# Routing one group later, row transposes in four pieces, and plain loads on SyncE's queue, in an attention-then-experts kernel

## The chip, the cores and the metric

The kernel runs on one core of a Trainium2 chip. The metric is the device time of one execution in microseconds (us). Engines are called as the profile calls them: PE is TensorE, DVE is VectorE, ACT is ScalarE, POOL is GpSimd, SP is SyncE. SP computes nothing here; it issues DMAs and waits for semaphores. A "q" behind an engine's name in a row (SPq, PEq) means its instruction queue.

## The reference

```python
u, v: (8, 2496, 256)   z: (8, 2496, 64)          # float32
scores = (1 / S) * z @ z.T                        # per batch, S = 2496
x = u * (max(scores, 0) ** 2 @ v)                 # 19968 tokens of 256
logits = (x / |x|) @ (emb / |emb|).T / tau        # 8 experts
e = argmax(logits);  gate = softmax(logits)[e]
out = gate * (max(x @ w1[e], 0) @ w2[e])          # w1: 256x1024, w2: 1024x256 for each expert
```

Products are made in float16 with each operand split in a high and a low part, so that three matmuls give nearly float32.

## The kernel before, in words

There are two stages. The first is attention with routing. It runs over 8 batches, in each over 5 groups of queries (512 tokens, the last one 448), and in each group over 20 steps, one for every 128 keys. A step of a group does up to three things: `scores` (L270, L271) makes a 128x512 block of scores on PE; ACT turns it into the squared relu `a` (L273, L274); `parts` (L307, L308) splits it on DVE into the float16 tile `hl`; and `values` (L362 to L371) multiplies `hl` with the split keys' values `vv` into the group's accumulators `acc`. The score matrix is symmetric, so blocks below the diagonal are not computed again: `parts` transposes `hl` by a DMA on SP's queue (L320 into `tt`, L322 into `joint`), and a later group reads it. `hl` has five buffers, and `parts` works two steps ahead of `values`. A step with its own scores takes PE 1.75 us, one that reads `tt` 1.31 us.

When a group's 20 steps are done, `route` returns a list of small functions, its routing. The main loop calls one of them after each step of the next group (`queue.pop(0)()`, L1101). In order they are: `gate_x` (L409, x = acc * u), `square` (L420), `root`, `scale`, `split` (L446, L447: x as high and low float16 into `row`), a DMA transpose of all rows of the group (L450), `logits` (L464, 16 small matmuls on PE into `pt`), `norms` and `top` (L468 on, DVE reads `pt`), `exps`, `gates`, `rank` (PE), `place`, and `scatters` (L532, four indirect DMAs on POOL's queue, which write each token's row into `xs`, sorted by expert). Before the change the first function is called right behind the group, splits end after step 5 of the next group, logits come after step 11, their first reading by DVE after step 13 and the scatters after step 18.

The accumulators of group g lie in two PSUM banks, `a0` and `a1` for an even group, `a2` and `a3` for an odd one. `pt`, the logits of group g, takes the first of the same group's banks (`bank`, L404), after `gate_x` has emptied it; the group g + 2 accumulates in it next.

During a batch, the loop also prepares the next one: `ahead` (L1009) loads parts of z and v for their largest values (`scan_load`), and z for its split (`z_load`, `z_split`, `z_copy`); `v_load` loads v four steps before `v_split` needs it. `weights` (L558) turns each expert's weights into split float16: two loads of 1 MB (L563, L564), a scale, four `part`s, two stores of 1 MB (L627) into `wsd`. These plain loads and stores go through POOL's queue; only those of the first group go through SP's (`loader`, L101).

The second stage takes the sorted rows in slots of 256 or 128 tokens of one expert: SP loads weights (L919, L921) and row transposes (L896), PE makes the up and down products, POOL scatters the results (L970). Routing of the last groups goes on beside its first slots.

PE's instructions stay in the order in which the program names them. The other engines' order, and that of SP's queue in the first stage, is made by a planner, which simulates the program with costs of its own and issues on every engine what is ready first there. On the chip each engine then keeps that order: an instruction that waits holds up all behind it on its engine.

Of the kernel before, what the change touches and what calls it, by code (L numbers as in the profile page):

```python
# [19 lines left out]
P = 128  # L20
TA, TB = 256, 128
ROW = 260
ROWT = 320
EUP = 14
VAHEAD = 4
LOOK = 3
# [19 lines left out]
def relu2_attention_then_moe(ctx, tc, zT, u, v, emb, tau, w1, w2, ident, tri, iota_e, out):  # L46
# [51 lines left out]
    assert SP * DQ == ZSCANS * SCAN * P and DQ % ZSCANS == 0 and SP % VSCANS == 0  # L98
    scan = {}

    def loader(b, g=0):  # L101
        return nc.sync if b == 0 and g == 0 else nc.gpsimd

    def scan_load(b, what, i, eng=None):

        t = wk.tile([P, SCAN], F32, name="scan", tag="scan", bufs=2)
        if what == "z":
            src = zT[b, i * (DQ // ZSCANS):(i + 1) * (DQ // ZSCANS), :]
        else:
            src = v[b, i * (SP // VSCANS):(i + 1) * (SP // VSCANS), :]  # L110
        (eng or loader(b)).dma_start(t, src.rearrange("a c -> (a c)").rearrange("(p w) -> p w", p=P))
        scan[b, what, i] = t

    def scan_max(b, what, i):
# [58 lines left out]
    def z_load(b, c0):  # L173
        zt = zpool.tile([P, ZC], F32, name="zt", tag="zt", bufs=3)
        c1 = min(c0 + ZC, SP)
        m = P if b == 0 else DQ
        loader(b).dma_start(zt[:m, :c1 - c0], zT[b, :m, c0:c1])
        zraw[b, c0] = zt

    def z_split(b, c0):  # L180
# [14 lines left out]
    def z_copy(b, c0, c1):  # L195
        z1, z2 = Zs[b]
        c = slice(c0, c1)
        loader(b).dma_start(z1[DQ:P, c], z2[0:DQ, c])
        loader(b).dma_start(z2[DQ:P, c], z1[0:DQ, c])

    vraw = {}

    def v_load(b, s):
        vt = wk.tile([P, D], F32, name="vt", tag="vt", bufs=VAHEAD + 2)
        loader(b).dma_start(vt, v[b, s * P:(s + 1) * P, :])  # L205
        vraw[b, s] = vt

    VC = 4
# [19 lines left out]
    def v_split(b, s):  # L228
        vt = vraw.pop((b, s))
        vv = vring.tile([P, 2 * D], F16, name="vv", tag="vv")  # L230
        k = scan[b, "cv"]
        if s == NST - 1:

            lo, hi = slice(0, DQ), slice(DQ, P)
            vh = wk.tile([P, D], F16, name="vh", tag="vh", bufs=1)
            nc.scalar.activation(vv[lo, 0:D], vt[lo], AF.Copy, scale=k[lo])
            nc.vector.tensor_copy(vv[lo, D:], vv[lo, 0:D])
            nc.scalar.activation(vh[hi], vt[hi], AF.Copy, scale=k[hi])
            nc.vector.scalar_tensor_tensor(vv[hi, 0:D], vt[hi], k[hi], vh[hi], op0=ALU.mult, op1=ALU.subtract)
            nc.vector.memset(vv[hi, D:], 0.0)  # L240
        else:
            nc.scalar.activation(vv[:, 0:D], vt, AF.Copy, scale=k)
            nc.vector.scalar_tensor_tensor(vv[:, D:], vt, k, vv[:, 0:D], op0=ALU.mult, op1=ALU.subtract)
        Vs[b, s] = vv
# [128 lines left out]
    def u_load(b, g):  # L373
        t0, n = groups[g]
        ut = rt.tile([P, 4, D], F32, name="ut", tag="ut")
        m = n // P
        loader(b, g).dma_start(ut[:, :m, :], u[b, t0:t0 + m * P, :].rearrange("(j p) d -> p j d", p=P))
        if n > m * P:
            for h in range(2):
                loader(b, g).dma_start(ut[h * DQ:(h + 1) * DQ, m, :], u[b, t0 + m * P:t0 + n, :])  # L380
        return ut

    obs = [cst.tile([P, 9, E], BF16, name=f"ob{i}") for i in range(2)]
    rows = [cst.tile([P, 4, ROWT], F32, name=f"row{i}") for i in range(2)]
    for t in obs:
        nc.gpsimd.memset(t, 0.0)
    for t in rows:
# [2 lines left out]
    def route(b, g, acc, ut):  # L390
# [48 lines left out]

        def split(j):  # L440
            up = loc["up"][:, j:j + 1]
            if j == 0:
                with tc.issue_after(loc["gate"]):
                    nc.vector.memset(row[:, :, D:D + 2], 0.0)
            hi, lo = row16[:, j, 0:D], row16[:, j, D:2 * D]
            nc.scalar.activation(hi, x[:, j, :], AF.Copy, scale=up)  # L446
            nc.vector.scalar_tensor_tensor(lo, x[:, j, :], up, hi, op0=ALU.mult, op1=ALU.subtract)  # L447
            if j == nj - 1:
                loc["rt"] = rt.tile([P, 4, ROWT * 2 // P, P], F16, name="rowt", tag="x", bufs=1)
                nc.sync.dma_start_transpose(loc["rt"].rearrange("p j i t -> p (j i) t"), row16.rearrange("p j c -> p (j c)"))  # L450

        def splits(j0):
            def f():
                for j in range(j0, min(j0 + 2, nj)):
                    split(j)
            return f

        def logits():
            pt = loc["pt"] = bank()
# [69 lines left out]
        def scatter(j):  # L529
            def f():  # L530
                m = min(P, n - j * P)
                put = nc.gpsimd.indirect_dma_start(  # L532
                    xs[:, :], bass.IndirectOffsetOnAxis(ap=loc["dsti"][:m, j:j + 1], axis=0),
                    row[:m, j, 0:ROW], None)
                for o in (o for old in puts.values() for o in old):
                    tc.declare_no_dep(put.ins, o, reason="each token has one row of xs")
                puts.setdefault(b, []).append(put.ins)
            return f
# [5 lines left out]
        def both(*fs):  # L544
# [4 lines left out]

        assert nj == 4  # L550
        none = lambda: None
        two = lambda j: both(lambda: square(j), lambda: square(j + 1))
        start = [gate_x, both(fold, two(0)) if n == 512 else none, two(2) if n == 512 else both(fold, two(0))]
        return start + [none if n == 512 else two(2), root, both(scale, splits(0)), splits(2)] + [none] * 5 + [
            logits, none, both(norms, top), exps, gates, rank, place, scatters]


    def weights(e):  # L558
        loc = {}

        def load():
            loc["wr"] = (wp.tile([P, W1], F32, name="wr1", tag="wr1"), wp.tile([P, W2], F32, name="wr2", tag="wr2"))
            nc.gpsimd.dma_start(loc["wr"][0].rearrange("p (k f) -> p k f", k=2), w1[e].rearrange("(k p) f -> p k f", p=P))  # L563
            nc.gpsimd.dma_start(loc["wr"][1].rearrange("p (k d) -> p k d", k=NF), w2[e].rearrange("(k p) d -> p k d", p=P))  # L564

        def maxes(k):
            def f():
# [22 lines left out]
        def powers():  # L590
            dg = loc["dg"]
            pm2 = psM.tile([P, 512], F32, name="pm", tag="m")
            nc.tensor.matmul(pm2[:, 0:2], ones_f[0:2, :], dg, start=True, stop=True)
            pw = sml.tile([P, 2], F32, name="pw")
            nc.vector.tensor_copy(pw, pm2[:, 0:2])
            up = sml.tile([P, 2], F32, name="wup")
            dn = sml.tile([P, 2], F32, name="wdn")
            for k, a in ((0, 2), (1, 9)):
                nc.vector.tensor_scalar(up.bitcast(I32)[:, k:k + 1], pw.bitcast(I32)[:, k:k + 1], -1.0,
                                        float((254 + a) << 23), op0=ALU.mult, op1=ALU.add)  # L600
                nc.vector.tensor_scalar(dn.bitcast(I32)[:, k:k + 1], pw.bitcast(I32)[:, k:k + 1], 1.0,
                                        float(-(a << 23)), op0=ALU.mult, op1=ALU.add)
            tail = sml.tile([P, 4], F32, name="tail")
            nc.gpsimd.memset(tail, 0.0)
            nc.vector.tensor_tensor(tail[:, 0:1], dn[:, 0:1], dn[:, 1:2], op=ALU.mult)
            nc.gpsimd.dma_start(wsd[e, :, WR1 + 2 * W2:], tail.bitcast(F16))
            loc["up"] = up

        def part(i):

            def f():
                k = i // 2
                wr = loc["wr"][k]
                W = (W1, W2)[k]
                if i % 2 == 0:
                    loc["wo"] = wp.tile([P, 2 * max(W1, W2)], F16, name="wo", tag="wo")
                wo = loc["wo"]
                u = loc["up"][:, k:k + 1]
                c = 512
                for o in range((i % 2) * (W // 2), (i % 2 + 1) * (W // 2), c):  # L620
                    m = min(c, (i % 2 + 1) * (W // 2) - o)
                    src = wr[:, o:o + m]
                    nc.scalar.activation(wo[:, o:o + m], src, AF.Copy, scale=u)
                    nc.vector.scalar_tensor_tensor(wo[:, W + o:W + o + m], src, u, wo[:, o:o + m],
                                                   op0=ALU.mult, op1=ALU.subtract)
                if i % 2 == 1:
                    nc.gpsimd.dma_start(wsd[e, :, 2 * k * W1:2 * (k * W1 + W)], wo[:, 0:2 * W])  # L627
            return f

        return [load, lambda: None, maxes(0), maxes(1), scales, powers] + [part(i) for i in range(4)]  # L630
# [402 lines left out]
    for i, (b, g, q, s) in enumerate(steps):  # L1033
# [75 lines left out]
            slot_weights()  # L1109
            slot_first()  # L1110
        if q == NST - 1:
            while queue:
                queue.pop(0)()
            queue = route(b, g, accs.pop((b, g)), uts.pop((b, g)))
            if b == B - 2 and g == NG - 1 and KA:
                queue.append(table_a)
            queue.pop(0)()
        if own:
            if nd + LOOK - 1 < len(direct):
# [98 lines left out]
```

## Time and profile before

| | us |
|---|---|
| median of 3 runs | 2328.91 (2327.23 to 2343.7) |
| the profiled execution | 2333.62 |
| its span, first to last instruction | 2331.8 |
| attention with routing, 25.4 to 1476.5 | 1451.1 |
| idle time of PE in it | 156.0 |
| of it, logits waiting for the transposed rows | 111.5 |
| expert stage, 1505 to 2331 | 826.0 |
| idle time of PE in it | 7.7 |

The profile is of one execution. Times in rows are in us from the start of the span unless marked ns. A row of a group of instructions has line, engine, operation, output and inputs by the program's names and a count. A row of a wait has who waited, for whom, total us, times, longest. A row of the timeline has start, duration, engine, line and operation; in brackets the idle time of the engine before it and what ended that. DMA rows tell packets, megabytes and, for each queue (q1 is SP's, q0 is POOL's), the time its packets took as a share of 16 DMA engines.

### The profile page before, as it was taken

The page shows a single profiled execution, that of the slowest core. Times are in us where ns is not written, and L with a number is a line of the kernel's source. Part 1 is how long each engine was busy: PE and PEld are TensorE (multiplying, and loading weights), DVE is VectorE, ACT ScalarE, POOL GpSimd, SP SyncE. Part 2 cuts the span into 40 slices and gives each one's busy share as a digit, 9 for nine tenths or more (in the row PEclk, how much of TensorE's full clock was granted, in tenths as well). Part 3 has the DMA queues.
Part 4 walks back from the last instruction along what each step waited for, and adds up shares of the span by engine and source line. Part 5 has one row for each costly group of instructions (what it writes and reads, how often), then busy time and mean ns, then how long its engine had stood idle before and what let it go on. Part 6 is the DMA issues. An engine that isn't in the chain of part 4 may idle for free. (4 is left out here: it accounts for less than half of the span.)

```text
span 2331.8 us, 50551 instructions
## 1 busy us (share of the span) xinstructions
PE 2140.6 (92%) x19210; PEld 1804.3 (77%) x19210; DVE 1353.3 (58%) x4024; ACT 1032.5 (44%) x2131; POOL 569.6 (24%) x739
## 2 busy tenths in 40 slices
PE   6998877997999898897899999899999999999999
PEld 4786656776777677776687777788888888888888
DVE  7876755875777776675687765343333333333333
ACT  6566544753755655654565654222222222222211
POOL 2132224133224215212322211122121211112121
PEclk9999988998999999998899999999999999999999
DMA  7968976996996996886897786352332333237574
GB/s 191 211 152 197 185 127 146 178 219 120 181 211 144 180 208 173 166 185 122 179 202 142 152 187 108 100 153 50 90 89 68 92 83 74 47 82 205 137 189 129
DMA packets 622743, 341.17 MB, mean 146 GB/s; under 512 B 578229, under 2 KB 583998, under 8 KB 614304
## 3 DMA queue, kind: packets, MB, share of 16 engines
q1 hardware_dynamic: 578336, 191.77, 45.0%
q0 software_dynamic: 43872, 145.74, 22.3%
q8 instruction: 152, 2.49, 0.5%
q14 instruction: 95, 0.78, 0.1%
q10 hardware_dynamic: 288, 0.39, 0.1%
HBM read 273.46 MB, written 59.60 MB: 143 GB/s over the span
## 5 line engine op out<-in xcount | busy, mean ns | idle before, releaser
L273 ACT ACTIVATE a<-sc 128x512 f32<-128x512 f32 (+1 forms) x480 | 269.6, 562 | 346.6 <-PE sc L271 272.6
L970 POOL DMA_INDIRECT out_dram<-ot,me x159 | 155.1, 975 | 684.8 <-DVE ot L969 644.3
L274 ACT ACTIVATE a<-a 128x512 f32<-128x512 f32 (+1 forms) x480 | 286.3, 597 | 12.5
L532 POOL DMA_INDIRECT xs<-row,dsti x160 | 173.8, 1086 | 481.8 <-ACT a L273 266.1
L364 PE MATMUL acc<-vv,tt 128*128 128x256 f16 x1152 | 276.1, 278 | 0.0
L362 PE MATMUL acc<-vv,tt 128*128 128x256 f16 x1152 | 276.0, 278 | 0.0
L963 PE MATMUL po<-w,hh 128*128 128x256 f16 x928 | 253.2, 273 | 0.0
L965 PE MATMUL po<-w,hl 128*128 128x256 f16 x928 | 253.1, 273 | 0.0
L964 PE MATMUL po<-w,hh 128*128 128x256 f16 x928 | 253.1, 273 | 0.0
L270 PE MATMUL sc<-z 128*128 128x512 f16 (+1 forms) x480 | 180.1, 375 | 11.8 <-ACT a L273 8.7
L969 DVE TENSOR_SCALAR ot<-po,me,w 128x256 f32<-128x256 f32 x116 | 58.3, 540 | 218.4 <-PE po L965 215.8
L366 PE MATMUL acc<-vv,tt 128*128 128x256 f16 x1152 | 182.3, 277 | 0.0
L271 PE MATMUL sc<-z,z 128*128 128x512 f16 (+1 forms) x480 | 180.4, 376 | 0.0
L963 PEld LDWEIGHTS <-hh 128*128 128x128 f16 x1272 | 124.6, 98 | 14.5 <-issue 0.2
L965 PEld LDWEIGHTS <-hl 128*128 128x128 f16 x1272 | 124.5, 98 | 14.5
L964 PEld LDWEIGHTS <-hh 128*128 128x128 f16 x1272 | 124.6, 98 | 14.3
L366 PEld LDWEIGHTS <-tt 128*128 128x128 f16 x1152 | 114.8, 100 | 15.1
L362 PEld LDWEIGHTS <-tt 128*128 128x128 f16 x1152 | 114.5, 99 | 14.9
L364 PEld LDWEIGHTS <-tt 128*128 128x128 f16 x1152 | 114.6, 99 | 14.6
L464 PE MATMUL pt<-e,rowt 128*128 128x16 f16 x640 | 22.6, 171 | 111.5 <-DMA rowt<-row 111.5
L464 PEld LDWEIGHTS <-rowt 128*128 128x128 f16 x640 | 21.0, 99 | 117.1 <-DMA rowt<-row 116.5
L205 POOL DMA_DIRECT2D vt<-in_v_dram x140 | 77.3, 560 | 95.0 <-DMA wr<-in_w_dram 20.6
(5262 smaller groups left out, 5936.0 us busy)
## 6 DMA issues: line engine op xcount, KB each, us to landing
w<-wsd SPq DMA_DIRECT2D x64, 1026.0 KB
wa<-wsd SPq DMA_DIRECT2D x46, 1024.0 KB
w<-wsd SPq DMA_DIRECT2D x42, 1024.0 KB
wb<-wsd SPq DMA_DIRECT2D x24, 1026.0 KB
vt<-in_v_dram POOLq DMA_DIRECT2D x140, 128.0 KB
scan<-in_v_dram POOLq DMA_DIRECT2D x56, 320.0 KB
wr<-in_w_dram POOLq DMA_DIRECT2D x16, 1024.0 KB
wsd<-wo POOLq DMA_DIRECT2D x16, 1024.0 KB
```

The source lines that it names most:

```text
L270: nc.tensor.matmul(sc[:, :n], z1[:, ss], z1[:, t0:t0 + n], start=True, stop=False)
L271: nc.tensor.matmul(sc[:, :n], z1[:, ss], z2[:, t0:t0 + n], start=False, stop=True)
L273: state["at"] = nc.scalar.activation(a[:, :n], sc[:, :n], AF.Relu, scale=2.0 ** -SHIFT).ins
L274: nc.scalar.activation(a[:, :n], a[:, :n], AF.Square)
L362: nc.tensor.matmul(outs[j], piece(ph, j), vh, start=first and j % 2 == 0, stop=False, skip_group_check=True)
L364: nc.tensor.matmul(outs[j], piece(ph, j), vl, start=False, stop=False, skip_group_check=True)
L366: nc.tensor.matmul(outs[j], piece(pl, j), vl if last else vh, start=False, stop=ends, skip_group_check=True)
L532: put = nc.gpsimd.indirect_dma_start(xs[:, :], bass.IndirectOffsetOnAxis(ap=loc["dsti"][:m, j:j + 1], axis=0), row[:m, j, 0:ROW], None)
L963: nc.tensor.matmul(o, hh[:, f, t], wh, start=(f == 0), stop=False)
L964: nc.tensor.matmul(o, hh[:, f, t], wl, start=False, stop=False)
L965: nc.tensor.matmul(o, hl[:, f, t], wh, start=False, stop=(f == NF - 1))
L970: put = nc.gpsimd.indirect_dma_start(out, bass.IndirectOffsetOnAxis(ap=me.bitcast(U32)[:, j, 1:2], axis=0), ot[:, j, :], None, bounds_chec ...
```

## The change

Four things change.

1. The routing list gets six entries more: the first function does nothing, `gate_x` comes after the next group's step 0, one `square` or one `split` per step in place of two, splits after steps 8 to 11, logits after step 18, their reading (`norms`, `top`) after step 19, and `exps` to `scatters` after the end of that group and the first four steps of the one after. The lists of two groups are therefore merged entry by entry: while a new group's routing begins, the end of the older one's is called in the same steps.
2. Each `split` issues the transpose of its own 128 tokens (128x512 float16), so there are four per group in place of one of 128x2560. Rows in SBUF shrink from 320 to 260 words, the transposed rows get a buffer of their own in place of sharing one with `x`, and the clearing of two words of each row (L444) is left out.
3. `loader` is gone: scans, z, v, u, the copies of z, the weights' loads and stores go to SP's queue. The scatters stay on POOL's.
4. Clearing half of the last v tile of a batch (L240) moves from DVE to POOL.

```diff
-ROWT = 320
...
-    def loader(b, g=0):
-        return nc.sync if b == 0 and g == 0 else nc.gpsimd
...
-        (eng or loader(b)).dma_start(t, src.rearrange("a c -> (a c)").rearrange("(p w) -> p w", p=P))
+        (eng or nc.sync).dma_start(t, src.rearrange("a c -> (a c)").rearrange("(p w) -> p w", p=P))
...
-        loader(b).dma_start(zt[:m, :c1 - c0], zT[b, :m, c0:c1])
+        nc.sync.dma_start(zt[:m, :c1 - c0], zT[b, :m, c0:c1])
...
-        loader(b).dma_start(z1[DQ:P, c], z2[0:DQ, c])
-        loader(b).dma_start(z2[DQ:P, c], z1[0:DQ, c])
+        nc.sync.dma_start(z1[DQ:P, c], z2[0:DQ, c])
+        nc.sync.dma_start(z2[DQ:P, c], z1[0:DQ, c])
...
-        loader(b).dma_start(vt, v[b, s * P:(s + 1) * P, :])
+        nc.sync.dma_start(vt, v[b, s * P:(s + 1) * P, :])
...
-            nc.vector.memset(vv[hi, D:], 0.0)
+            nc.gpsimd.memset(vv[hi, D:], 0.0)
...
-        loader(b, g).dma_start(ut[:, :m, :], u[b, t0:t0 + m * P, :].rearrange("(j p) d -> p j d", p=P))
+        nc.sync.dma_start(ut[:, :m, :], u[b, t0:t0 + m * P, :].rearrange("(j p) d -> p j d", p=P))
...
-    rows = [cst.tile([P, 4, ROWT], F32, name=f"row{i}") for i in range(2)]
+    rows = [cst.tile([P, 4, ROW], F32, name=f"row{i}") for i in range(2)]
...
         def split(j):
             up = loc["up"][:, j:j + 1]
-            if j == 0:
-                with tc.issue_after(loc["gate"]):
-                    nc.vector.memset(row[:, :, D:D + 2], 0.0)
             hi, lo = row16[:, j, 0:D], row16[:, j, D:2 * D]
             nc.scalar.activation(hi, x[:, j, :], AF.Copy, scale=up)
             nc.vector.scalar_tensor_tensor(lo, x[:, j, :], up, hi, op0=ALU.mult, op1=ALU.subtract)
-            if j == nj - 1:
-                loc["rt"] = rt.tile([P, 4, ROWT * 2 // P, P], F16, name="rowt", tag="x", bufs=1)
-                nc.sync.dma_start_transpose(loc["rt"].rearrange("p j i t -> p (j i) t"), row16.rearrange("p j c -> p (j c)"))
-
-        def splits(j0):
-            def f():
-                for j in range(j0, min(j0 + 2, nj)):
-                    split(j)
-            return f
+            if j == 0:
+                loc["rt"] = rt.tile([P, 4, 4, P], F16, name="rowt", tag="rowt", bufs=1)
+            nc.sync.dma_start_transpose(loc["rt"][:, j, :, :], row16[:, j, 0:2 * D])
...
-        two = lambda j: both(lambda: square(j), lambda: square(j + 1))
-        start = [gate_x, both(fold, two(0)) if n == 512 else none, two(2) if n == 512 else both(fold, two(0))]
-        return start + [none if n == 512 else two(2), root, both(scale, splits(0)), splits(2)] + [none] * 5 + [
-            logits, none, both(norms, top), exps, gates, rank, place, scatters]
+        one = lambda f, *a: lambda: f(*a)
+        begin = [none, gate_x, none, both(fold, one(square, 0)), one(square, 1), one(square, 2), one(square, 3), root, scale]
+        begin += [one(split, j) for j in range(nj)]
+        begin += [none] * (NST - 1 - len(begin))
+        return begin + [logits, both(norms, top), exps, gates, rank, place, scatters]
...
-            nc.gpsimd.dma_start(loc["wr"][0].rearrange("p (k f) -> p k f", k=2), w1[e].rearrange("(k p) f -> p k f", p=P))
-            nc.gpsimd.dma_start(loc["wr"][1].rearrange("p (k d) -> p k d", k=NF), w2[e].rearrange("(k p) d -> p k d", p=P))
+            nc.sync.dma_start(loc["wr"][0].rearrange("p (k f) -> p k f", k=2), w1[e].rearrange("(k p) f -> p k f", p=P))
+            nc.sync.dma_start(loc["wr"][1].rearrange("p (k d) -> p k d", k=NF), w2[e].rearrange("(k p) d -> p k d", p=P))
...
-                    nc.gpsimd.dma_start(wsd[e, :, 2 * k * W1:2 * (k * W1 + W)], wo[:, 0:2 * W])
+                    nc.sync.dma_start(wsd[e, :, 2 * k * W1:2 * (k * W1 + W)], wo[:, 0:2 * W])
...
         if q == NST - 1:
-            while queue:
-                queue.pop(0)()
-            queue = route(b, g, accs.pop((b, g)), uts.pop((b, g)))
+            new = route(b, g, accs.pop((b, g)), uts.pop((b, g)))
             if b == B - 2 and g == NG - 1 and KA:
-                queue.append(table_a)
+                new.append(table_a)
+            assert len(queue) <= len(new)
+            queue = [(lambda fs=fs: [f() for f in fs]) for fs in
+                     [[q[i] for q in (queue, new) if i < len(q)] for i in range(len(new))]]
             queue.pop(0)()
```

More of the change, by code (lines that the diff above doesn't have):

```diff
@@ L376, in u_load @@
         m = n // P
-        loader(b, g).dma_start(ut[:, :m, :], u[b, t0:t0 + m * P, :].rearrange("(j p) d -> p j d", p=P))
+        nc.sync.dma_start(ut[:, :m, :], u[b, t0:t0 + m * P, :].rearrange("(j p) d -> p j d", p=P))
         if n > m * P:
             for h in range(2):
-                loader(b, g).dma_start(ut[h * DQ:(h + 1) * DQ, m, :], u[b, t0 + m * P:t0 + n, :])
+                nc.sync.dma_start(ut[h * DQ:(h + 1) * DQ, m, :], u[b, t0 + m * P:t0 + n, :])
         return ut
     obs = [cst.tile([P, 9, E], BF16, name=f"ob{i}") for i in range(2)]
-    rows = [cst.tile([P, 4, ROWT], F32, name=f"row{i}") for i in range(2)]
+    rows = [cst.tile([P, 4, ROW], F32, name=f"row{i}") for i in range(2)]
     for t in obs:
@@ L533, in f @@
                     xs[:, :], bass.IndirectOffsetOnAxis(ap=loc["dsti"][:m, j:j + 1], axis=0),
-                    row[:m, j, 0:ROW], None)
+                    row[:m, j, :], None)
                 for o in (o for old in puts.values() for o in old):
@@ L605, in powers @@
             nc.vector.tensor_tensor(tail[:, 0:1], dn[:, 0:1], dn[:, 1:2], op=ALU.mult)
-            nc.gpsimd.dma_start(wsd[e, :, WR1 + 2 * W2:], tail.bitcast(F16))
+            nc.sync.dma_start(wsd[e, :, WR1 + 2 * W2:], tail.bitcast(F16))
             loc["up"] = up
```

## The prediction

> **What bounds the kernel now.** I read the page first, then the busy times by stage, then who TensorE (PE) waited for, then the stretch around the longest wait, then the DMA queues in single stretches.
>
> ```profile
> PE 2140.6 (92%) x19210; PEld 1804.3 (77%) x19210; DVE 1353.3 (58%) x4024; ACT 1032.5 (44%) x2131; POOL 569.6 (24%) x739
> ...
> 25.40:1476.50 1451.10, 1295.11 (x11135) 1046.57 (x11135) 1023.64 (x3398) 827.46 (x1778) 402.81 (x559) 0.94 0.83 167
> 403.90:438.50 34.60, 34.60 (x299) 27.68 (x298) 31.96 (x98) 26.52 (x55) 4.64 (x6) 1.00 0.98 177
> 1505.00:2331.00 826.00, 818.31 (x7886) 737.49 (x7882) 301.88 (x550) 184.27 (x310) 156.92 (x161) 1.00 0.42 105
> ```
>
> The second to fourth rows are stretches: length, busy time of PE, weight loads, DVE, ACT, POOL, then granted clock. The expert stage (last row) is PE at full clock; nothing of the change can shorten it. Attention with routing (second row) leaves PE idle for 1451.1 - 1295.1 = 156 us and at 0.94 of its clock. The third row is one group of 512 tokens without a disturbance: PE has no gap, though DVE is busy for 32.0 of 34.6 us. So PE sets the pace and what it waits for is time.
>
> ```profile
> PE pt L464 <- DMA rowt<-row: 111.5, 18, 14.6
> PE sc L270 <- ACT a L273: 8.7, 3, 5.1
> ...
> PE acc L362 <- DVE hl__13742 L307: 5.8, 1, 5.8
> PE acc L362 <- DVE hl__19770 L307: 2.6, 1, 2.6
> PE acc L362 <- DVE hl__3162 L307: 2.2, 1, 2.2
> ```
>
> Total, times, longest. 111.5 of the 156 us are the logits (L464) waiting for the transposed rows, in 18 of 40 groups. This is the worst of them:
>
> ```profile
> 322.38 10.13 SPq L450 DMA_TRANSPOSE rowt<-row  x1
> 324.84 0.71 POOL L563 DMA_DIRECT2D wr<-in_w_dram  x1
> 345.01 0.60 PE L464 MATMUL pt<-e,rowt 128*128 128x16 f16 x16 [14.64 <-DMA rowt<-row]
> ...
> 345.00:350.70 5.70, 5.69 (x37) 3.58 (x38) 3.56 (x16) 2.38 (x6) 0.54 (x1) 0.50 0.09 21
> 350.70:356.40 5.70, 5.70 (x56) 4.91 (x54) 3.75 (x9) 3.87 (x9) 0.53 (x1) 1.00 0.57 105
> ```
>
> SyncE needs 10.1 us to issue one transpose, and the rows are there 22.6 us after the issue began, with a 1 MB weight load on POOL's queue in between. The wait has an echo: the next 5.7 us run at half clock, 37 matmuls in place of 56, which costs (5.7/2) = 2.9 us.
>
> **The change part by part.** *Loads onto SyncE's queue.* Three stretches of the DMA view, and a transpose with no load beside it:
>
> ```profile
> DMA packets 946, 1.56 MB, mean 156 GB/s; under 512 B 596, under 2 KB 596, under 8 KB 946
> ...
> q0 software_dynamic: 418, 1.43, 80.6%
> q1 hardware_dynamic: 528, 0.13, 21.4%
> ...
> DMA packets 2145, 0.53 MB, mean 266 GB/s; under 512 B 2145, under 2 KB 2145, under 8 KB 2145
> ...
> DMA packets 191, 1.43 MB, mean 359 GB/s; under 512 B 16, under 2 KB 16, under 8 KB 16
> ...
> 1401.16 3.64 SPq L450 DMA_TRANSPOSE rowt<-row  x1
> 1406.36 0.60 PE L464 MATMUL pt<-e,rowt 128*128 128x16 f16 x16 [3.73 <-DMA rowt<-row]
> ```
>
> The first three rows are 377 to 387 us: POOL's loads (q0) and SyncE's transposes (q1) together, and the transposes get 0.13 MB in 10 us. The fourth is 64 to 66 us, transposes alone: 266 GB/s. The fifth is 1520 to 1524 us, loads alone, on SyncE's queue: 359 GB/s. Without a load the 640 KB of rows land 5.2 us after their issue (last two rows), with one 22.6. So two queues that share the engines cost the transposes far more than the loads' own time. In one queue a transpose stands behind a 1 MB load for 1.05/359 = 2.9 us, behind a pair (L563, L564) for 5.8. The expert stage above already has 1 MB loads and row transposes on SyncE's queue and PE idles for 7.7 of its 826 us. I take it that the mixing ends. The Trainium skill (DMA: Bandwidth & Descriptors, Issuing engines are not separate DMA queues) speaks against this part: transfers from any engine end on the same 16 DMA engines and interleave, so another issuer saves sequencer time alone. By that rule the sum would be the second rival's; by the rows above, where loads and transposes that follow each other keep their rates, it is the one below.
>
> *Four transposes per group, logits later.*
>
> ```profile
> L450 SPq DMA_TRANSPOSE rowt<-row x40: 3003/3811/10128, 74.4 to 1490.1; - x40
> L322 SPq DMA_TRANSPOSE joint<-hl__811 x1: 1217/1217/1217, 69.0 to 69.0; - x1
> L177 SPq DMA_DIRECT2D zt<-in_zT_dram x10: 328/408/1382, 1.2 to 38.6; - x10
> SPq L450 <- DVE row L447: 128.2, 12, 17.9
> ...
> 82.48 0.38 PE L270 MATMUL sc<-z 128*128 128x512 f16 x1
> 84.23 0.38 PE L270 MATMUL sc<-z 128*128 128x512 f16 x1
> ...
> 324.52 0.60 PE L366 MATMUL acc<-vv,tt 128*128 128x256 f16 x4
> 325.83 0.60 PE L366 MATMUL acc<-vv,tt 128*128 128x256 f16 x4
> ```
>
> A joint transpose has the shape of the new ones (128x512, f16): 1.22 us of SyncE. Four are 4.9 us against a median of 3.8, so 1.1 us more per group, off the path. Some 400 loads by the code (70 scans, 70 zt, 140 vt, 28 copies, 55 u, 40 for weights) at 0.41 us add 165 us to SyncE over 1451 us. A step of PE is 1.75 us with scores (82.48 to 84.23) and 1.31 without. Splits now end in step 11 and logits come in step 18: seven steps, 9.2 to 12.3 us, against six before. The last piece is ready about 5.2 - (3.64 - 1.22) = 2.8 us after its issue, or 8.6 behind a pair of weight loads. SyncE already stands still for splits that DVE makes late (fourth row, up to 17.9 us); now loads are queued behind that wait, vt first, four steps before ACT wants it. Splits and loads are ordered by the same planner, so I charge it nothing and keep it for a rival. POOL's queue keeps the scatters alone, and PE waits for none of them before the expert stage. Result: the 111.5 us go. The echoes with them: at most 18 x 2.9 = 52, at least 0; the mean wait is only 111.5/18 = 6.2, so I take 34. I keep a tenth of both, 15 us, for groups where a split is late and a weight pair stands ahead.
>
> *A new wait.* The logits and the accumulators of the group after share a bank (`a0` or `a2`). So far the logits are read six steps before the bank is wanted; now they are written in step 18, read by DVE during step 19, and the next group's first matmul follows.
>
> ```profile
> 85.97 0.55 PE L464 MATMUL pt<-e,rowt 128*128 128x16 f16 x16
> 88.26 0.19 DVE L469 TENSOR_TENSOR lg<-pt,lg 128x32 f32<-128x32 f32 x1
> ...
> 828.52 0.59 PE L464 MATMUL pt<-e,rowt 128*128 128x16 f16 x16 [3.14 <-DMA rowt<-row]
> 834.21 0.19 DVE L469 TENSOR_TENSOR lg<-pt,lg 128x32 f32<-128x32 f32 x1
> ...
> 1504.66 0.55 PE L464 MATMUL pt<-e,rowt 128*128 128x16 f16 x16
> 1505.47 0.19 DVE L469 TENSOR_TENSOR lg<-pt,lg 128x32 f32<-128x32 f32 x1
> 1505.72 0.28 PE L939 MATMUL ph__21616<-xt,wa 128*128 128x256 f16 x1 [0.51 <-DVE lg L469]
> ```
>
> From the logits' end to the end of the last read: 1.9 us in the first group, 0.45 in the last, 5.3 at 828 us, one of the three longest of 40. The wait exists: the last row is PE waiting for this read. With a step of 1.31 to 1.75 us in between, the 40 delays taken one by one would leave 20 to 31 us over 38 group starts; I take 25, and 3 for echoes. Ends: 0, and 38 x (5.3 - 1.3) = 152.
>
> *The rest.* The transposes of hl free five buffers in turn, and DVE has waited for them where they were slow (the L307 rows in the second fence; L270 waits behind the same, by way of ACT). These PE waits are 8.7 + 5.8 + 2.6 + 2.2 = 19.3 us; a buffer comes round after five steps, 8.7 us, so a 2.9 us load ahead of it is covered and a pair is not: I credit 12, ends 0 and 19. Forty small memsets leave DVE, eight go to POOL, gate_x starts a step later: hidden by the 2.6 us per undisturbed group that DVE is free, and by POOL being idle for three quarters of the span; without cover under 10 us. The routing of the last groups ends six pops later in the expert stage, where DVE is busy for 302 of 826 us: nothing.
>
> Sum: -111.5 - 34 + 15 + 25 + 3 - 12 = -114.5. The profiled execution took 2333.6 us (span 2331.8), 4.7 over the median of 2328.9: 2333.6 - 114.5 - 4.7 = 2214 us.
>
> **The rivals.** *The mixing stays* (0.16). If the DMA engines handle a load and a transpose badly whatever queue they came by, rowt keeps its slowness; the step more (1.3) and the shorter last issue (3.8 - 1.2 = 2.6) give 3.9 us per wait, at most 18 x 3.9 = 70 and, as short waits have less to give, about 55, with 17 of the echoes. Against 28 for the bank that leaves -44: 2285 us. For it speaks that the scatters stay on POOL; against it the expert stage.
>
> *SyncE's queue becomes the wait* (0.11). Every 1 MB transfer (two loads and two stores for each of 8 experts, 32) holds back a transpose or a vt load that then is wanted: 32 x 2.9 = 93 us more, with echoes some 110: about 2325 us, no change. For it: SyncE's long standstills; against: 8.7 us of cover for hl, seven steps for rowt.
>
> *The bank wait is long everywhere* (0.17), which ends slower. At a group's end DVE has the next group's first parts and gate_x to do, and if it reads the logits as late as at 828 us each time, PE stands 4.0 us at 38 starts, 152 us, with echoes at 2.4 each 91 more: 2214 - 28 + 243 = 2429 us. It decides the sign from about 3 us per start on (114 us, and the echoes set in). For it: DVE is busy 92% of the undisturbed group, and DVE's order is fixed in advance. Against it: 26 of the 40 delays are under 2 us, and some of the long ones (828 us among them) follow a PE wait that is to go.
>
> *More than forecast* (0.06): no bank wait, all hl waits gone, no remainder: 2214 - 15 - 28 - 7 = 2164 us.
>
> **How the numbers follow.** The forecast has 0.50; its own range is 2165 (no bank wait, no remainder, all hl waits gone) to 2270 (twice the bank wait, no hl credit, echoes of 15 in place of 34). Faster by over 1% (below 2306), which about is what a measurement of this kernel can tell: 0.50 + 0.06 + 0.15 of the first rival = 0.71; within 1%, 0.10 of the queue rival and 0.01 of the first: 0.11; slower, the bank rival and the last 0.01 of the queue's: 0.18. The range that leaves two in ten out reaches from the best case through the queue rival to 2345.
>
> **What would show it.** Right: L464 no longer leads PE's waits; clock near 1.00 over attention; idle of PE under 60 us, led by L362 waiting for L469 at group starts with some 0.7 us each; four transposes of about 1.2 us each. Wrong: L464 still waits with loads in flight (first rival); L307 waiting for tt, or ACT for vt, in most groups (second); L362 waiting for L469 by 4 us at every start (third).

## The result and the profile after

The kernel after takes 2199.21 us (median; 2190.66 to 2204.09), the kernel before on the same chip 2329.89 (2327.23 to 2343.7). The ratio is 0.942, 95% interval 0.938 to 0.947: 5.8% faster. The forecast was 2214 us with "faster over 1%" as the likeliest outcome, so number and side were right. Several of its steps were not, and the experiments below show that the reason I put first, the mixing of loads and transposes, is one of two parts of the change that each remove most of the wait alone.

The profiled execution took 2204.1 us against 2333.6 before: 129.5 us less, where the working had a sum of 114.5. First the page's busy times for the kernel after:

```profile
PE 2111.8 (96%) x19210; PEld 1790.4 (81%) x19210; DVE 1327.8 (60%) x3976; ACT 1030.6 (47%) x2131; POOL 329.3 (15%) x344
```

Then its stretches, in the columns of the prediction's rows (length, PE, weight loads, DVE, ACT, POOL, granted clock, DMA share, GB/s): attention, one undisturbed group (the fourth of its batch, which makes fewer blocks of scores than the group in the prediction), expert stage.

```profile
24.20:1355.80 1331.60, 1270.35 (x11130) 1035.11 (x11130) 996.18 (x3337) 825.08 (x1777) 163.57 (x165) 0.98 0.84 179
...
308.40:338.00 29.60, 29.36 (x275) 25.21 (x275) 21.91 (x85) 18.34 (x45) 4.20 (x4) 1.00 0.96 211
...
1355.80:2202.30 846.50, 836.06 (x8069) 752.96 (x8066) 315.84 (x600) 193.79 (x333) 162.84 (x167) 1.00 0.43 108
```

Attention is 1451.1 - 1331.6 = 119.5 us shorter. It falls in two parts: PE's idle time went from 156.0 to 1331.6 - 1270.4 = 61.3 us (94.7 less), and PE's busy time from 1295.1 to 1270.4 (24.8 less) for the same matmuls, as the granted clock rose from 0.94 to 0.98. For the expert stage the same cut has to be taken in the kernel before:

```profile
1476.50:2331.80 855.30, 839.97 (x8063) 755.34 (x8061) 313.79 (x587) 193.33 (x332) 161.78 (x166) 0.99 0.43 107
```

That is 855.3 - 846.5 = 8.8 us, which I had put at nothing (PE's idle time in it 15.3 to 10.4, its busy time 840.0 to 836.1); the start (25.4 to 24.2) gives 1.2. Together 119.5 + 8.8 + 1.2 = 129.5.

What PE waits for in the kernel after (total, times, longest):

```profile
PE pm L495 <- DVE ob L472: 20.0, 18, 2.8
PE acc L358 <- DVE lg L456: 15.5, 10, 2.8
PE pm L128 <- DVE smz L126: 6.9, 1, 6.9
PE pm L128 <- DVE smv L126: 4.5, 1, 4.5
PE acc L358 <- DVE hl__19833 L303: 4.4, 1, 4.4
PE acc L358 <- DVE hl__11270 L303: 4.1, 1, 4.1
PE acc L358 <- DVE hl__3236 L303: 3.3, 1, 3.3
PE acc L358 <- DVE hl__13878 L303: 3.3, 1, 3.3
```

No row has the logits (now L451) waiting for the transposed rows: the wait of 111.5 us is gone altogether. At the top stand two waits that the kernel before did not have among its costs: the rank matmuls for the one-hot rows `ob` that DVE makes after the gates (20.0 us), and the first matmul of a group for DVE's read of the logits in the shared bank (15.5 us, the new wait of the forecast). The issues of the row transposes (shortest, median, longest in ns, then first and last start):

```profile
L443 SPq DMA_TRANSPOSE rowt<-row x160: 1188/1227/2802, 75.4 to 1379.5; - x160
```

And from the order of time, one route's transpose and its logits:

```profile
316.03 1.23 SPq L443 DMA_TRANSPOSE rowt<-row  x1
...
335.91 0.55 PE L451 MATMUL pt<-e,rowt 128*128 128x16 f16 x16
```

Each of the four takes 1.23 us in the median, as forecast. The route is that of the same group as the prediction's worst case. There the rows were issued at 322.4 and wanted at 345.0 - 14.6 = 330.4, 8 us later; here they are issued from 316.0 on and wanted 19.9 us later.

And a DMA stretch of 10 us, 326 to 336 us, with transposes of `hl` and a 1 MB weight load in flight (the four row transposes were issued just before it), to be laid beside the prediction's stretch of 156 GB/s:

```profile
DMA packets 3442, 2.24 MB, mean 224 GB/s; under 512 B 2654, under 2 KB 3185, under 8 KB 3441
...
q1 hardware_dynamic: 3441, 2.23, 102.9%
```

All of it is in SyncE's queue now. By their size the small packets are mainly the transposes' (alone they made 0.53 MB of 2145, some 250 bytes each): 2654 of them in 10 us, where the mixed stretch had 528 for the transposes.

### The profile page after: what moved, and what is told of

Its sections match the earlier page's. It is cut to its first block, busy times and chain, and to the rows that moved or that the text cites. A ratio compares the mean times of both kernels' runs of the same rounds, so it can differ in the third digit from the quotient of the medians.

```text
span 2202.3 us, 50859 instructions
## 1 busy us (share of the span) xinstructions
PE 2111.8 (96%) x19210; PEld 1790.4 (81%) x19210; DVE 1327.8 (60%) x3976; ACT 1030.6 (47%) x2131; POOL 329.3 (15%) x344
## 4 chain that ended last, share of the span: by engine, by line
PE 75%; DVE 10%; DMA 9%; ACT 4%; issue 2%; SPq 1%; DVEq 0%; POOL 0%; POOLq 0%; ACTq 0%
PE acc L358 10%; PE acc L362 10%; PE acc L360 10%; PE po L951 6%; PE po L952 6%; PE po L953 6%; PE sc L266 3%; PE sc L267 3%; DMA scan<-in_v_dram 2%; DVE x L405 1%; ACT a L269 1%; DMA zt<-in_zT_dram 1%; ACT a L270 1%; DMA vt<-in_v_dram 1%; DVE wo L612 1%
## 5 line engine op out<-in xcount | busy, mean ns | idle before, releaser
L519 POOL DMA_INDIRECT xs<-row,dsti x160 | 168.4, 1053 | 1097.6 <-ACT row L439 361.1
L439 ACT ACTIVATE row<-x,up 128x256 f16<-128x256 f32 x160 | 71.2, 499 | 52.2 <-DVE up L427 44.8
L951 PE MATMUL po<-wb,hh 128*128 128x256 f16 x344 | 93.8, 273 | 0.0
L953 PE MATMUL po<-wb,hl 128*128 128x256 f16 x344 | 93.8, 273 | 0.0
```

Of the source, the lines that this page charges most:

```text
L519: put = nc.gpsimd.indirect_dma_start(xs[:, :], bass.IndirectOffsetOnAxis(ap=loc["dsti"][:m, j:j + 1], axis=0), row[:m, j, :], None)
L951: nc.tensor.matmul(o, hh[:, f, t], wh, start=(f == 0), stop=False)
L953: nc.tensor.matmul(o, hl[:, f, t], wh, start=False, stop=(f == NF - 1))
```

## The experiments

All ratios are to the kernel before on the same chip, with the 95% interval. Waits are PE's rows, as above; the hl sum adds all rows in which PE waits for the `hl` or `joint` of attention, or for `a`, which stands behind them.

### The loads alone

The kernel before, with every plain load and the weights on SyncE's queue; the other three lines of the weights (the second load, and the two that write the prepared weights back) change in the same way. One transpose per group and the logits stay as they were.

```diff
     def loader(b, g=0):
-        return nc.sync if b == 0 and g == 0 else nc.gpsimd
+        return nc.sync
...
-            nc.gpsimd.dma_start(loc["wr"][0].rearrange("p (k f) -> p k f", k=2), w1[e].rearrange("(k p) f -> p k f", p=P))
+            nc.sync.dma_start(loc["wr"][0].rearrange("p (k f) -> p k f", k=2), w1[e].rearrange("(k p) f -> p k f", p=P))
...
```

> The kernel before with one thing of the change: all plain loads and stores on SyncE's queue; one transpose per group and logits after step 11 stay. Theory (loads and transposes in two queues at once slow the transposes): PE's wait for rowt falls from 111.5 us to under 30, the longest L450 issue from 10.1 us to under 6, time 2215 to 2245 us. Rival (the later logits made the gain, the issuer is of no account): the wait stays over 80 us and the time is 2300 to 2335 us.

Measured: 2198.41 us (2193.97 to 2200.8), ratio 0.943 [0.936, 0.950]. PE's longest wait:

```profile
PE pt L464 <- DMA rowt<-row: 19.0, 11, 6.5
```

The issues of its transposes:

```profile
L450 SPq DMA_TRANSPOSE rowt<-row x40: 3039/3424/7846, 74.8 to 1357.5; - x40
```

This one part gives the whole gain of the change, more than I expected of it. The wait falls from 111.5 to 19.0 us with nothing else in the program changed; only the longest issue, 7.8 us, stays above the 6 I had. The splits end no earlier for it: in the median 9.2 us after the group's start (9.4 in the kernel before) and 8.4 us before the logits want their rows (8.6). What changed is the landing: in the groups that waited, the rows were there 4.9 to 8.8 us after their issue began, where the kernel before has 5.2 to 22.6. The Trainium skill (DMA: Bandwidth & Descriptors, Issuing engines are not separate DMA queues) says that issuing DMAs from several engines at once only saves the issuing sequencers' time. This run disagrees: the same transfers, by another issuer, are worth 5.7%, and the wait that goes is one for transposes whose issuer is SyncE in both kernels.

### The whole change without the loads

The kernel after, with the loads on POOL's queue again (`loader` and the four weight lines as before).

> The changed kernel with one thing undone: the loads and stores go through POOL's queue again; four transposes and late logits stay. Theory: PE waits for rowt again, 30 to 70 us in all, in the groups where weights are loaded, and for hl behind slow transposes; time 2260 to 2300 us. Rival (the issuer is of no account): no wait for rowt, 2195 to 2215 us.

Measured: 2244.34 us (2232.07 to 2252.61), ratio 0.964 [0.956, 0.971]. PE's two longest waits:

```profile
PE acc L361 <- DVE lg L459: 26.6, 13, 5.1
PE pm L498 <- DVE ob L475: 17.7, 18, 3.5
```

The issues of its transposes:

```profile
L446 SPq DMA_TRANSPOSE rowt<-row x160: 1188/1240/4442, 73.9 to 1410.2; - x160
```

Time as neither side had it, and no wait for the rows at all, where my theory wanted 30 to 70 us. So the later logits remove that wait also where loads and transposes are still mixed. The mixing costs something else: beside the kernel after, the bank wait is 11 us longer (26.6 against 15.5), and so is the hl sum (34.7 against 23.3).

### The later routing alone

The kernel before, with the new routing list and the two queues merged; the loads on POOL and one transpose per group.

```diff
-        start = [gate_x, both(fold, two(0)) if n == 512 else none, two(2) if n == 512 else both(fold, two(0))]
-        return start + [none if n == 512 else two(2), root, both(scale, splits(0)), splits(2)] + [none] * 5 + [
-            logits, none, both(norms, top), exps, gates, rank, place, scatters]
+        begin = [none, gate_x, none, both(fold, one(square, 0)), one(square, 1), one(square, 2), one(square, 3), root, scale]
+        begin += [one(split, j) for j in range(nj)]
+        begin += [none] * (NST - 1 - len(begin))
+        return begin + [logits, both(norms, top), exps, gates, rank, place, scatters]
```

> The kernel before with the new routing list alone (logits after step 18, lists of two groups merged); one transpose per group, loads on POOL's queue. Theory: one step more between splits and logits takes 1.3 to 1.75 us from each of 18 waits, the bank wait gives it back: wait for rowt 75 to 105 us, time 2300 to 2340 us. Rival (the later logits made the gain): wait for rowt under 30 us, time under 2240 us.

Measured: 2246.74 us (2244.98 to 2253.89), ratio 0.964 [0.957, 0.971]. PE's two longest waits:

```profile
PE acc L362 <- DVE lg L469: 31.2, 14, 5.2
PE pm L508 <- DVE ob L485: 19.1, 12, 4.7
```

What the trace has on the transposes' tile, the issues and who waited for them:

```profile
L450 SPq DMA_TRANSPOSE rowt<-row x40: 3047/3996/13999, 75.0 to 1429.6; - x40
...
  PE pt L464: 0.6, 1
```

And in order of time the route with the longest issue:

```profile
736.82 0.76 POOL L564 DMA_DIRECT2D wr<-in_w_dram  x1
...
737.82 14.00 SPq L450 DMA_TRANSPOSE rowt<-row  x1
...
766.71 0.45 PE L464 MATMUL pt<-e,rowt 128*128 128x16 f16 x12
```

My theory fell here; the wait is what the rival had, the time a little longer. The transposes are as slow as ever, with one issue of 14.0 us behind a weight load, and PE waits 0.6 us for all of them, since the logits of that route come 28.9 us after the issue began. The step that I had got wrong is where the data becomes ready. I had moved the splits back with their places in the list, to step 11, and so left nearly the same distance to the logits. But the list's place binds PE's instructions; what DVE and ACT have to do for it is fitted in earlier. Over the 39 groups in each trace whose routing runs beside a later group, the last split ends in the median 9.4 us after the group's start in the kernel before, 10.3 in this one and 10.2 in the kernel after, though its place is six steps later in the last two. From there to the moment the logits are wanted, 8.6 us in the median and 1.3 at the least had been left; now it is 20.8 here and 21.5 (at least 10.4) in the kernel after.

This kernel gains 84 us where the wait it removes is 111.5: the bank and the rank matmuls take 31.2 + 19.1 = 50.3 us back, and less goes into echoes.

### Weights alone, and loads on another queue

Is it the eight pairs of 1 MB transfers, or POOL's queue in particular? Three variants of the kernel before, with one transpose and the old routing: only the weights' loads and stores on SyncE; the same on ACT's queue; all loads except the first group's, and the weights, on ACT's queue. The diff is of the third; the first two leave `loader` alone, and the first has `nc.sync` in the four lines of the weights.

```diff
-        return nc.sync if b == 0 and g == 0 else nc.gpsimd
+        return nc.sync if b == 0 and g == 0 else nc.scalar
...
-                    nc.gpsimd.dma_start(wsd[e, :, 2 * k * W1:2 * (k * W1 + W)], wo[:, 0:2 * W])
+                    nc.scalar.dma_start(wsd[e, :, 2 * k * W1:2 * (k * W1 + W)], wo[:, 0:2 * W])
```

> The kernel before with the experts' weights alone (two loads and two stores of 1 MB and a small store each) on SyncE's queue; the smaller loads stay on POOL's. If the 1 MB transfers are what the transposes collide with: waits for rowt over 10 us are gone, the total is under 45 us, time 2225 to 2260 us. If all loads matter alike, weights are 34 of about 80 MB of them, less than half: total wait over 65 us, time over 2275 us.

> The kernel before with the experts' weights (two loads, two stores of 1 MB and a small one each) on ScalarE's hardware queue. With them on SyncE's queue the wait for rowt was 83.2 us, 9.2 at the longest, against 111.5 and 14.6 on POOL's. If a second queue beside SyncE's is what slows the transposes, whoever makes its descriptors: waits of 13 us and more stay, total 100 to 130 us, time 2310 to 2350 us. If it is POOL's way of making descriptors: longest wait about 9 us, total 75 to 95 us, time 2280 to 2305 us.

> The kernel before with all plain loads and stores (but the first group's) on ScalarE's hardware queue in place of POOL's; nothing else changed. In e1, with all of them on SyncE's queue, PE waited 19.0 us for rowt, 6.5 at the longest. If any second queue beside the transposes slows them: wait for rowt 75 to 130 us, longest over 10 us, time 2290 to 2400 us (ScalarE itself is held up by issuing and by waits of the loads). If only POOL's queue does: wait for rowt under 35 us, longest under 8 us.

Measured: 2294.73 us (2286.96 to 2309.4), ratio 0.987 [0.979, 0.995]; 2299.49 (2291.56 to 2313.11), 0.989 [0.985, 0.993]; 2278.42 (2273.76 to 2284.57), 0.977 [0.971, 0.982]. PE's wait for the rows, first in the kernel with the weights on SyncE,

```profile
PE pt L464 <- DMA rowt<-row: 83.2, 17, 9.2
```

then with the weights on ACT's queue,

```profile
PE pt L464 <- DMA rowt<-row: 91.4, 21, 10.9
```

then with all loads on ACT's queue:

```profile
PE pt L464 <- DMA rowt<-row: 82.8, 22, 9.0
```

The first meets its second expectation: the 1 MB transfers are not it alone. With them on SyncE three quarters of the wait stay, and it takes the small loads too (19.0 us) to remove the rest. The second meets the expectation for POOL's way of making descriptors in total and in time, with a longest wait (10.9 us) somewhat over its 9. The third met neither: the time is better than one side had it and the wait longer than the other allowed.

These totals mix two things. The splits end at different times: with all loads on ACT's queue ACT issues them besides its own work, and the last splits end 12.3 us after the group's start against 9.4. An estimate from the timestamps of each trace takes the two apart: had the rows landed 5.2 us after their issue began, as in the prediction's transpose without a load, what is left of each wait is the part of slow transposes. It comes to 93 of the 111.5 us in the kernel before, 10 of 19.0 with all loads on SyncE, and 38 of 82.8 with all on ACT; with the weights alone moved, to 43 of 83.2 (SyncE) and 68 of 91.4 (ACT). On SyncE the weights alone thus take away about half of the slow part. The slowest landing among the waits is 22.6 us with the loads on POOL, 14.6 on ACT and 8.8 on SyncE. So a second queue of ACT's slows the transposes as well, and POOL's does so more. Each figure is from one trace, and why POOL's is the worse stays open.

### The bank and rank waits: logits two steps sooner

The kernel after, with the logits two steps sooner and an empty entry ahead of the rank matmuls.

```diff
-        begin += [none] * (NST - 1 - len(begin))
-        return begin + [logits, both(norms, top), exps, gates, rank, place, scatters]
+        begin += [none] * (NST - 3 - len(begin))
+        return begin + [logits, both(norms, top), exps, gates, none, rank, place, scatters]
```

> The changed kernel with logits after step 16 in place of 18, and an empty entry between gates and rank, so that rank comes five steps after the logits as in the kernel before. Theory (in the changed kernel PE pays for reading the logits too late: 15.5 us at the bank, 20.0 us at rank): both waits under 5 us together, no wait for rowt, time 2155 to 2175 us. Rival (DVE is the limit there and the wait moves to hl): hl waits grow by the same, time 2190 to 2205 us.

Measured: 2189.09 us (2185.88 to 2196.01), ratio 0.941 [0.936, 0.946]. Its longest waits of PE beside those for the scales:

```profile
PE sc L266 <- ACT a L269: 5.8, 2, 3.8
...
PE acc L358 <- DVE hl__11248 L303: 4.2, 1, 4.2
...
PE acc L358 <- DVE hl__19811 L303: 3.8, 1, 3.8
PE acc L358 <- DVE hl__13717 L303: 3.7, 1, 3.7
```

Bank and rank waits, 35.5 us, are gone but for one of 2.2. The median is 10 us lower, but the ratios to the kernel before, 0.941 and 0.942, do not tell the two kernels apart. The hl sum went from 23 to 41 us: half of what was removed came back as waits for hl. That is the direction that the rival had, not its whole size.

### Four transposes or one

The kernel after, with one transpose of 128x2560 per group as before, when the last split is done; the rows are 320 words wide again, with the memset of two of them in each group.

```diff
-            if j == 0:
-                loc["rt"] = rt.tile([P, 4, 4, P], F16, name="rowt", tag="rowt", bufs=1)
-            nc.sync.dma_start_transpose(loc["rt"][:, j, :, :], row16[:, j, 0:2 * D])
+            if j == nj - 1:
+                loc["rt"] = rt.tile([P, 4, ROWT * 2 // P, P], F16, name="rowt", tag="x", bufs=1)
+                nc.sync.dma_start_transpose(loc["rt"].rearrange("p j i t -> p (j i) t"), row16.rearrange("p j c -> p (j c)"))
```

> The changed kernel with one transpose of 128x2560 per group again in place of four (rows of 320 words, their two words cleared again); loads stay on SyncE's queue, logits stay late. Theory (with loads out of the other queue and 20 us between split and logits the number of transposes is of no account): 2190 to 2210 us, no wait for rowt. Rival (four pieces matter): waits for rowt or hl of 15 us and more, over 2215 us.

Measured: 2188.29 us (2183.22 to 2190.76), ratio 0.939 [0.934, 0.944]. The waits of PE:

```profile
PE pm L499 <- DVE ob L476: 17.8, 16, 2.2
PE acc L359 <- DVE lg L460: 16.2, 8, 5.3
...
PE acc L359 <- DVE hl__11253 L304: 2.3, 1, 2.3
```

The issues of the one transpose per group:

```profile
L447 SPq DMA_TRANSPOSE rowt<-row x40: 3051/4371/8809, 73.7 to 1359.0; - x40
```

No wait for the rows either, so the four are not needed for that. The single one is 11 us faster in the medians, with the hl sum at 13 us against 23, but the intervals of the two kernels overlap: that four cost anything is unclear.

### The parts together

The kernel before with the loads on SyncE, one transpose, the new list and the logits two steps sooner; then the same with six hl buffers in place of five (`bufs=6` at the two tiles `hl_`), beside the former once more.

> The kernel before with loads on SyncE's queue and logits after step 16 (rank five steps later), one transpose per group. Theory: no wait for rowt, bank and rank under 5 us together, time 2150 to 2175 us, the same as with four transposes within 10 us. Rival (the remaining 66 us of waits are DVE's load, whatever the routing's place): 2190 us or more.

> The kernel of e10 (loads on SyncE, logits after step 16, one transpose per group) with six buffers for hl in place of five. Of e10's 51 us of PE waits in attention 32 are for hl. Theory (DVE waits for a buffer whose transpose has not landed: landing takes up to 16 us after the split, a buffer comes round after five steps, 8.7 us): a sixth step of cover takes most of them: hl waits 5 to 15 us, time 2145 to 2165 us. Rival (DVE itself is late, its own work being 32 of 34.6 us): hl waits stay over 25 us, time within 8 us of e10.

> The kernel of e10 once more, on the chip of e11, so that five and six buffers stand side by side: 2165 to 2185 us.

Measured: 2174.34 us (2167.41 to 2180.25), ratio 0.933 [0.928, 0.939], and in the second measurement 2171.78, 0.931 [0.927, 0.936]; with six buffers 2164.22 (2158.42 to 2167.25), 0.927 [0.922, 0.932]. PE's waits with six buffers:

```profile
PE sc L270 <- ACT a L273: 5.7, 2, 3.7
...
PE acc L366 <- DVE hl__9098 L308: 3.5, 1, 3.5
```

This last one beats both kernels, by 35 us the kernel after (measured on another chip; by the ratios, 0.927 against 0.942). A sixth buffer lowers the hl sum only from 30 and 35 (the kernel ahead of it, twice) to 25 us, where I expected 5 to 15, so the number of buffers is part of that wait but not most of it.

### The runs side by side

Attention's length and PE's waits in it, us; each from its own trace.

| Kernel | Median | Attention | rowt | Bank | Rank | hl sum |
|---|---|---|---|---|---|---|
| before | 2329.9 | 1451.1 | 111.5 | - | - | 29 |
| after | 2199.2 | 1331.6 | - | 15.5 | 20.0 | 23 |
| loads alone | 2198.4 | 1322.2 | 19.0 | - | 1.0 | 26 |
| after, loads on POOL | 2244.3 | 1359.4 | - | 26.6 | 17.7 | 35 |
| later routing alone | 2246.7 | 1380.4 | 0.6 | 31.2 | 19.1 | 37 |
| after, logits two sooner | 2189.1 | 1316.3 | 1.9 | - | 2.2 | 41 |
| after, one transpose | 2188.3 | 1313.4 | - | 16.2 | 17.8 | 13 |
| all parts, six hl | 2164.2 | 1295.7 | 1.9 | - | 2.0 | 25 |

## Why the prediction was right and wrong

**The 111.5 us go: right in size; the reason was right for most of them, but it was not the only way.** I let them go because the mixing ends, and kept 15 us back. They went without a remainder. By the estimate above slow transposes make 93 of them, as in the prediction's worst case; the rest is splits that ended so late, 1.3 to 5.1 us before the logits were wanted, that even a quick transpose did not make it, or issues that came late. The loads alone leave 19.0 us, near my remainder; the later routing alone, with the transposes as slow as before, leaves 0.6.

**"Splits now end in step 11 and logits come in step 18: seven steps, 9.2 to 12.3 us, against six before": wrong.** This is the step that failed. The last split ends some 10 us into the group in both kernels, and 21.5 us in the median are left in place of 8.6. The first rival rests on the same step: it gave the mixing kernel 3.9 us more per wait and 2285 us, where the later routing with the mixing kept has 2244 and no wait for the rows.

**The echoes: -34 and +3 forecast, -24.8 measured** as PE's busy time in attention. The clock went to 0.98, not to 1.00. I take it that the 35.5 us of new waits bring echoes of their own: in the run that is without them (the logits two steps sooner) the clock is 0.99 and PE is busy for 1262.2 us, though its hl waits are longer.

**The bank wait: +25 forecast, 15.5 measured,** 10 times and at most 2.8 us. It is there, of the mechanism foretold. With the loads still on POOL it is 26.6 and 31.2 us. The rival with 4 us at each of 38 starts (152 us) is out by a factor of ten.

**The rank matmuls: missed, 20.0 us.** The prediction has no term for them. The empty entry between logits and norms is gone from the list, so the rank matmuls follow the logits by four steps in place of five, and DVE's chain in between does not always fit. The run with an empty entry put back has 2.2 us; it has the logits two steps sooner as well, so which of the two did it is not shown apart.

**The waits for hl: -12 forecast, -5.6 measured.** The rows I had listed add up to 19.3 us, but all rows of this kind to 28.9 before and 23.3 after. The waits for `a` (8.7 us) are gone, and those for hl itself went from 20.2 to 23.3. The queue rival, for which these would have grown much more, did not come: DVE's waits for a buffer that is still being transposed are at most 5.3 us, against 8.3 before, and SyncE's waits ahead of the row transposes, with all their releasers, add up to 131.3 us, where the kernel before has 318.2. From the waits of DVE and of SyncE's queue in the kernel after:

```profile
DVE hl__13878 L303 <- DMA tt<-hl__13717: 5.3, 1, 5.3
```

and

```profile
SPq L443 <- DVE row L440: 12.5, 3, 10.7
```

**Not foreseen, in favour: the scale pieces and the expert stage.** PE's waits for the scales of z, v and the weights were longer in the kernel before:

```profile
PE pm L132 <- DVE smz L130: 9.0, 3, 6.9
...
PE pm L132 <- DVE pw L595: 7.5, 2, 3.9
...
PE pm L132 <- DVE smv L130: 5.5, 1, 5.5
...
PE ph__21569 L939 <- DMA wa<-wsd: 4.3, 1, 4.3
...
PE ph__33110 L939 <- DMA wa<-wsd: 3.3, 1, 3.3
```

All rows for scales sum to 28.8 us before and 14.8 after. Of the 28.8, 13.0 lie in attention, and in the kernel after none does: 13 us. The last two rows are waits for the experts' weights, at 1499.8 and 2264.3 us; the kernel after has 0.2 and 1.2 in their place. PE's idle time in the expert stage is 4.9 us less in all, and the other 3.9 of the 8.8 are its busy time at a clock of 1.00 in place of 0.99.

For PE's idle time in attention this adds up: -111.5 + 15.5 + 20.0 - 5.6 - 13.0 = -94.6, measured -94.7. That my sum came out near is in part luck: a remainder that did not stay (-15) and gains that I missed (-13.0, -8.8, and -1.2 at the start) lay opposite a wait that I missed (+20), and the bank, the echoes and the hl waits were each off by 6 to 10 us.

**The two parts do not add.** The loads alone gain 133 us, the later routing alone 84, the whole change 131, and both parts with the one transpose 141. Once the loads are on SyncE, the later logits buy the last 19.0 us of waits and cost 35.5 in new ones (34.0 with one transpose), and the kernels come out alike: 2198.4, 2199.2 and 2188.3 us, with intervals of the ratio that overlap. That the loads would do it all was in reach of the prediction's own rows; I did not ask what each part is worth without the other.

**The issuer.** The prediction set the Trainium skill's statement (DMA: Bandwidth & Descriptors, Issuing engines are not separate DMA queues), that another issuer saves sequencer time alone, against its rows and went by the rows; the loads alone, at 2198.4 us, bear that out. It named the second rival as the sum of that rule; an issuer of no account is rather the case of the first, where the mixing stays (2285 us).

## What to carry to other kernels

Where a planner fits the work of the side engines in, the slack of a wait runs from the moment the data is really ready in the trace to the place of the instruction that wants it, so take it from timestamps, not from the list's steps. When two parts of a change remove the same wait, price each with the other already in: the second brings little, and its side costs (here a bank and a shorter chain) stay in full. And bulk loads that share the engines with small transposes on which PE waits are worth putting in the transposes' own queue before anything is rescheduled.

## What the runs showed of the hardware

**A second queue beside the transposes slows them.** Their rows landed up to 22.6 us after the issue with loads on POOL's queue, 14.6 on ACT's and 8.8 on SyncE's own. The prediction's stretch moved 156 GB/s with two queues, and the stretch of the kernel after 224 GB/s with all in one; each is one stretch. With the weights on ACT's queue, six microseconds behind a weight load (326 to 332 us; the small loads are still POOL's, q0) look like this in the trace's DMA view:

```profile
DMA packets 874, 1.68 MB, mean 279 GB/s; under 512 B 492, under 2 KB 492, under 8 KB 873
...
q0 software_dynamic: 185, 0.51, 51.5%
q10 hardware_dynamic: 271, 1.05, 47.0%
q1 hardware_dynamic: 417, 0.10, 21.2%
```

The transposes (q1) get 417 packets beside 456 of the loads' (185 + 271, q10 being ACT's), and in the prediction's stretch 528 beside 418, though a packet of theirs is some 250 bytes and one of the loads' 3 to 4 KB. Alone they had made 2145 packets in 2 us. This looks like turns taken packet by packet, and the Trainium skill (DMA: Bandwidth & Descriptors, Queues, rings and completion order) has the same rule: each DMA engine goes round the queues it has work for and changes between them at packets. The counts fit it, but no run varied the packets' size, and no run shows that the trace's packets are the skill's, so it is not shown to be the cause; nor does it say why POOL's stretch moves only 156 GB/s in all and this one 279.

**A small transpose is not cheaper to issue in proportion.** 128x512 takes 1.23 us of SyncE in the median and 128x2560 3.4 to 4.4 us in the medians of the kernels above, so four small ones (4.9 us) need more of SyncE than one large.
